# Row order of the left tokens' first-layer values, and the shape of their stores

## The chip, the cores and the metric

The kernel runs on one core of a Trainium2 chip. The core has five engines with instruction queues of their own: PE (TensorE, matrix products), ACT (ScalarE), DVE (VectorE), POOL (GpSimd) and SP (SyncE, which here only issues DMAs), and 16 DMA engines that carry the transfers. Work between the engines is ordered by semaphores. The metric is the device time of one execution, in microseconds.

## The reference

Inputs are q, k and v, each 8 batches x 8 heads x 576 positions x 64 values in float32, and two weight matrices. Attention is computed twice, once over positions averaged in groups of four and once over a band of seven positions, and the two are added. The 4608 tokens of 512 values then go through two layers:

```python
attn_out = out_up + out_local                  # [B, H, S, D]
x = attn_out.transpose(0, 2, 1, 3).reshape(B * S, H * D)   # 4608 x 512
h = x @ w_in                                   # 512 -> 2048
g = h - np.tanh(h)
out = (g @ w_out).astype(np.float32)           # 2048 -> 512, 4608 rows of 2 KB
```

## The kernel before

The attention works on pairs of heads, four pairs to a batch, and leaves its result transposed in `xT` (128 channels by tokens) with the 576 tokens of a batch ordered by (c, g), where token = 4 g + c, c from 0 to 3 and g from 0 to 143. The two layers work on blocks, one block to a batch. A block takes the first 128 values of g, that is 512 tokens. The other 16 values of g, 64 tokens to a batch (`LEFT`), are the *left tokens*: rows 512 to 575 of the batch. Those of two batches are put together into 128 tokens, and handled once for each pair m of batches, four times in all.

First layer of the left tokens (`left1`, e = 0 to 3): L809 makes 16 matmuls into one PSUM bank, four groups of 128 channels by 128 tokens; ACT takes the tanh (L820) into `u`, and DVE subtracts (L822) into `gL`, 128 channels by 16 groups by 128 tokens, in bf16. Those 128 tokens stand in the order (b, c, g): batch, c, g, as they come out of the bank.

Second layer of the left tokens (`left2`): L835 uses each group of `gL` as weights, 128 tokens by 128 channels, against `w_out`; so the order of the tokens in `gL` is the order of the partitions of the result. L846 copies that result, 128 partitions by 512 values, into the tile `keep0`. Then SP issues two stores (L851), one for each batch of the pair, of 64 partitions of `keep0`.

`keep0` is also the place where the second layer of the large blocks keeps a partial result. From the second block on that layer is done as seven products (`product`, L1003) of half the size with sums of blocks ahead of and behind them. The product n = 1 is copied from PSUM to `keep0` (`copy` at L1024, on ACT); the product n = 2 adds onto the same PSUM bank and so comes after that copy. Results of later products are added to `keep0` by POOL (L1074) and DVE (L1027). The copy at L1024 may write `keep0` only when the two stores at L851 have read it.

All operations are put into a list (`op`) with what they read and write; the order in which each engine gets them is a fixed list of turns (`TURNS`), written out in the kernel, and so are the choice of engine and the bank. Each engine works through its queue in order. SP's queue holds the loads of q, k and v (L326, L338, L350, L358, L365), the transposing DMAs (L529, L535, L760), the stores of y (L893) and those of `keep0` (L851). Buffers of loads come free when a cast or a sum on another engine has read them.

Of the kernel before, what the change touches and what calls it, by code (L numbers as in the profile page):

```python
# [10 lines left out]
ALU = mybir.AluOpType  # L11
# [3 lines left out]
class Plan:  # L15
# [13 lines left out]
    def op(self, eng, ns, fn, reads=(), writes=(), port=False, opens=None, uses=(),  # L29
           choice=None, rows=128, share=0.4):  # L30
        i = len(self.ops)
        deps = set()
        for key in reads:
            if key in self.last_write:
                deps.add(self.last_write[key])
        for key in writes:
            if key in self.last_write:
                deps.add(self.last_write[key])
            deps.update(self.readers.get(key, ()))
        for key in reads:  # L40
            self.readers.setdefault(key, set()).add(i)
        for key in writes:
            self.last_write[key] = i
            self.readers[key] = set()
        deps.discard(i)
        if opens and not isinstance(opens, list):
            opens = [opens]
        names = set(uses) | {o[0] for o in opens or ()}
        if choice:
            letter = self.engines[self.choices]  # L50
            self.choices += 1
            eng, ns, fn, port = next(a[:4] for a in choice if a[0][0] == letter)
        self.ops.append((fn, deps, opens or (), names))
        return i
# [34 lines left out]
def kernel(  # L89
# [11 lines left out]
    Dm, Dff = moe_w_in.shape  # L101
# [8 lines left out]
    NBLK, NR, LEFT = B, 3, S - 512  # L110
# [104 lines left out]
    def fixed(name, shape, dt, n=None, pool=const):  # L215
        if n is None:
            return pool.tile(shape, dt, name=name, tag=name)
        return [pool.tile(shape, dt, name=f"{name}{i}", tag=f"{name}{i}")
                for i in range(n)]
# [39 lines left out]
    u = fixed("u", [128, 512], FP32, 3)  # L259
# [7 lines left out]
    gL = fixed("gL", [128, N_FF, 2 * LEFT], BF16)  # L267
# [4 lines left out]
    op = P.op  # L272
    V, A, T, GP = nc.vector, nc.scalar, nc.tensor, nc.gpsimd

    def at(name):
        c = P.place[name]
        return bank[:, c[0]:c[-1] + 1, :]
# [523 lines left out]
    def left1(m, e):  # L801

        name, us = ("hl", m, e), (2 * m * (N_FF + 2) + 2 * N_FF + e) % 3
        s0, f0 = m % 2, 4 * e

        def mm(fs):
            for f in fs:
                for dc in range(N_DC):
                    T.matmul(at(name)[:, 0, 128 * f:128 * f + 128],  # L809
                             w_in_sb[:, dc, (f0 + f) * 128:(f0 + f) * 128 + 128],  # L810
                             xT[dc].rearrange("p (b c g) -> p b c g", b=NR, c=4)[:, s0:s0 + 2, :, 128:G],
                             start=(f == 0 and dc == 0), stop=(dc == N_DC - 1),
                             skip_group_check=True)
        for n in range(2):
            op("PE", 432, lambda n=n: mm(range(2 * n, 2 * n + 2)),
               reads=[("w_in", e)] + [("xs", s0 + i, j) for i in range(2) for j in range(N_DC)],
               writes=[("hld", m, e)] + (["turn1"] if n == 0 else []),
               opens=(name, TAIL if m == NBLK // 2 - 1 else DENSE) if n == 0 else None,
               uses=[name])
        op("ACT", 600, lambda: A.activation(out=u[us], in_=at(name)[:, 0, :], func=AF.Tanh),  # L820
           reads=[("hld", m, e)], writes=[("u", us)], uses=[name])
        op("DVE", 690, lambda: V.tensor_tensor(  # L822
            out=gL[:, f0:f0 + 4, :],
            in0=at(name)[:, 0, :].rearrange("p (f c) -> p f c", c=128),
            in1=u[us].rearrange("p (f c) -> p f c", c=128), op=ALU.subtract),
           reads=[("hld", m, e), ("u", us)], writes=[("gL", e)],
           uses=[name])

    def left2(m):

        name = ("yl", m)

        def mm(e):
            for fc in range(2 * e, 2 * e + 2):
                T.matmul(at(name)[:, 0, :], gL[:, fc, :], w_out_sb[:, fc, :],  # L835
                         start=(fc == 0), stop=(fc == N_FF - 1))
        for e in range(8):
            op("PE", 432, lambda e=e: mm(e),
               reads=[("w_out", e // 2), ("gL", e // 2)],
               writes=[("yld", m)] + (["turn2"] if e == 0 else []),  # L840
               opens=(name, TAIL if m == NBLK // 2 - 1 else DENSE) if e == 0 else None,
               uses=[name])
            if e % 2:
                yield
        op(None, 0, None, choice=[
            ("ACT", 590, lambda: A.copy(out=keep0, in_=at(name)[:, 0, :]), False),  # L846
            ("DVE", 680, lambda: V.tensor_copy(out=keep0, in_=at(name)[:, 0, :]), False, 0)],
           reads=[("yld", m)], writes=[("keep", 0)], uses=[name])
        for n in range(2):
            row = out[(2 * m + (n + m) % 2) * S + 512]  # L850
            op("SP", 450, lambda n=n, row=row: nc.sync.dma_start(  # L851
                out=bass.AP(tensor=row.tensor, offset=row.offset, ap=[[Dm, 4], [4 * Dm, LEFT // 4], [1, Dm]]),
                in_=keep0[LEFT * n:LEFT * n + LEFT, :]),
               reads=[("keep", 0)], writes=[("ylq", n)])
            op("DMA", 6.2 * LEFT, None, reads=[("keep", 0), ("ylq", n)])
# [231 lines left out]
    def second(kb):  # L1087
        if kb % 2:
            yield from left2(kb // 2)
        if not SEVEN[kb]:  # L1090
            for i in range(16):
                mm2(kb, i)
                yield
            return
        if kb == SEVEN.index(True):
            weight_sums()
        token_sums(kb, (0, 2))
        for n in ORDER7[kb == NBLK - 1]:
            yield from product(kb, n)
            if n < 3:  # L1100
                token_sums(kb, (2 * n - 1,))

    def dense(kb):
        steps = iter(()) if kb == 0 else second(kb - 1)
        count = 0 if kb == 0 else 16 + 12 * SEVEN[kb - 1] + 4 * (kb % 2 == 0)
        done, most = 0, 16 + 4 * (kb % 2)
        for i in range(most):
            if kb < NBLK:
                if i < 16:
                    mm1(kb, i)  # L1110
                else:
                    left1(kb // 2, i - 16)
            while done < (i + 1) * count // most:
                next(steps, None)
                done += 1
        for _ in steps:
            pass
# [66 lines left out]
    for p in range(NPAIR):  # L1184
# [16 lines left out]
        if p % NP == NP - 1:  # L1201
            b = p // NP
# [41 lines left out]
```

## Time and profile before

| | us |
|---|---|
| median of 3 runs | 329.01 |
| range of the runs | 328.72 to 329.73 |
| the profiled execution | 328.62 |
| its span, first to last instruction | 326.9 |
| PE busy | 304.2 (93%) |
| DVE busy | 263.4 (81%) |
| ACT busy | 210.5 (64%) |
| POOL busy | 177.7 (54%) |
| 8 stores at L851, issue on SP, each | 0.54 to 0.65 |
| 16 subtractions at L822, all | 10.7 |

The profile is of one execution. Its busy times come from the records of the instructions; a busy PE is not PE at its peak. A row of a group reads: line, engine, operation, what it writes and reads with shapes, count; then busy time in all and the mean in ns of one; then the engine's idle time before these instructions, and what ended it. A row of the chain reads: start, duration, what. "Landing" is the time from the issue of a DMA to the last arrival at its semaphore. PE's granted clock was 0.993 of full speed over the span.

### The profile page before, as it was taken

How to read it: one execution, taken by the hardware profiler on the slowest of the kernel's cores; microseconds unless marked ns; L12 is line 12 of the kernel's file. 1: busy time of each engine (PE TensorE's matmuls, PEld its weight loads, DVE VectorE, ACT ScalarE, POOL GpSimd, SP SyncE). 2: the span in 40 equal slices, each digit the busy share in tenths (PEclk: the TensorE clock that was granted, in tenths of full speed). 3: DMA queues.
4: the chain of work that ended last, by engine and by line, in shares of the span. 5: the costliest groups of instructions: out<-in, count | busy, mean ns of one | idle time of the engine just before them, and what ended most of it. 6: DMA issues, size and time to landing. Idle time of an engine off the chain costs nothing.

```text
span 326.9 us, 7852 instructions
## 1 busy us (share of the span) xinstructions
PE 304.2 (93%) x3001; PEld 201.6 (62%) x3014; DVE 263.4 (81%) x463; ACT 210.5 (64%) x380; POOL 177.7 (54%) x221
## 2 busy tenths in 40 slices
PE   7878999999998999899997999899997998999984
PEld 3675555555766665577676656755766457855773
DVE  3877886898899888999896689998995689746943
ACT  3877876578785797875754788478845774336400
POOL 6167873077684676838752969363931996410000
PEclk9989999999999999999999999999999999999999
DMA  7999999999995899997998796498948320540114
GB/s 222 266 268 230 231 214 166 266 233 209 251 267 145 167 259 257 287 204 187 218 256 167 173 238 190 126 247 136 334 126 137 68 54 39 80 150 0 66 32 128
DMA packets 114852, 59.62 MB, mean 182 GB/s; under 512 B 83968, under 2 KB 112128, under 8 KB 114816
## 3 DMA queue, kind: packets, MB, share of 16 engines
q1 hardware_dynamic: 109472, 52.77, 68.4%
q0 software_dynamic: 4704, 5.77, 9.9%
q10 hardware_dynamic: 640, 0.59, 0.6%
q8 instruction: 23, 0.38, 0.5%
q14 instruction: 13, 0.11, 0.1%
HBM read 44.04 MB, written 9.44 MB: 164 GB/s over the span
## 4 chain that ended last, share of the span: by engine, by line
PE 61%; DMA 19%; DVE 10%; ACT 3%; issue 3%; SPq 2%; POOL 0%; ACTq 0%; DVEq 0%
PE ps L782 28%; PE ps L1003 16%; DMA out_dram<-keep 7%; PE ps L809 4%; PE ps L835 4%; DMA vst<-in_v_dram 4%; PE ps L705 3%; DMA w_in_sb<-in_moe_w_in_dram 3%; DVE gT L797 2%; DVE gT L938 2%; PE ps L635 2%; DMA vr<-in_v_dram 2%; DMA st<-in_q_dram 2%; DMA sr<-in_k_dram 1%; PE ps L863 1%
## 5 line engine op out<-in xcount | busy, mean ns | idle before, releaser
L782 PE MATMUL ps<-xT,w_in_sb 128*128 128x512 bf16 x512 | 122.9, 379 | 1.8 <-DVE gT L797 0.8
L797 DVE TENSOR_TENSOR gT<-ps,u 128x512 bf16<-128x512 f32 x128 | 83.6, 683 | 20.8 <-ACT u L794 19.8
L794 ACT ACTIVATE u<-ps 128x512 f32<-128x512 f32 x128 | 73.5, 598 | 36.3 <-PE ps L782 32.6
L1003 PEld LDWEIGHTS <-gT 128*128 128x128 bf16 x672 | 64.3, 98 | 24.4 <-issue 7.1
L782 PEld LDWEIGHTS <-w_in_sb 128*128 128x128 bf16 x512 | 47.8, 98 | 49.3 <-issue 2.0
L1003 PE MATMUL ps<-w_out_sb,gT 128*128 128x256 bf16 x336 | 43.2, 273 | 5.6 <-ACT keep L1024 5.0
L1003 PE MATMUL ps<-Tw,gT 128*128 128x256 bf16 x336 | 42.1, 273 | 3.5 <-DVE gT L938 2.1
L484 POOL CAST qr<-st 128x512 bf16<-128x512 f32 x40 | 27.8, 703 | 17.5 <-DVE kt L546 4.2
L577 POOL TENSOR_TENSOR qkd<-half 128x288 bf16<-128x288 f32 x25 | 23.5, 941 | 20.4 <-DVE half L572 19.4
L656 ACT ACTIVATE E<-ps 128x912 bf16<-128x912 f32 x32 | 29.9, 935 | 3.5 <-PE ps L635 1.8
L723 DVE TENSOR_TENSOR ln<-ps,r 128x768 bf16<-128x768 f32 x32 | 30.5, 954 | 0.9
L1074 POOL TENSOR_TENSOR y<-y,keep 128x512 f32<-128x512 f32 x12 | 16.9, 1406 | 19.1 <-ACT y L1024 19.1
L691 DVE TENSOR_TENSOR E<-E,mask 128x1152 bf16<-128x1152 bf16 x27 | 24.5, 914 | 2.9 <-ACT E L656 1.6
L705 PEld LDWEIGHTS <-E 128*128 128x128 bf16 x576 | 22.1, 98 | 5.7 <-DVE E L691 1.3
L562 ACT COPY kt<-kq 128x576 bf16<-128x576 bf16 x20 | 23.8, 1189 | 2.0 <-DMA kq<-qr 2.0
L572 POOL TENSOR_TENSOR half<-kq 128x576 f32<-128x576 bf16 x13 | 17.1, 1315 | 14.6 <-ACT kq L557 6.9
L664 ACT ACTIVATE E<-ps 128x576 bf16<-128x576 f32 x32 | 20.9, 653 | 4.7 <-PE ps L651 4.7
L1024 ACT COPY y<-ps 128x512 f32<-128x512 f32 x19 | 11.1, 587 | 19.2 <-PE ps L1003 17.5
L938 DVE TENSOR_TENSOR gT<-gT 128x2048 bf16<-128x2048 bf16 x14 | 19.8, 1415 | 2.9 <-PE ps L1003 2.8
L741 POOL TENSOR_TENSOR xT<-lT 128x336 bf16<-128x336 bf16 (+1 forms) x24 | 17.4, 748 | 5.0 <-DMA lT<-ln 4.9
L705 PE MATMUL ps<-vw,E 128*128 128x65 bf16 x320 | 19.3, 195 | 0.6 <-DVE E L691 0.6
L705 PE MATMUL ps<-vpr,E 128*128 128x65 bf16 x128 | 16.5, 195 | 0.0
(122 smaller groups left out, 489.6 us busy)
## 6 DMA issues: line engine op xcount, KB each, us to landing
vst<-in_v_dram SPq DMA_DIRECT2D x64, 160.0 KB, 4.9
st<-in_k_dram SPq DMA_DIRECT2D x32, 256.0 KB, 3.4
st<-in_q_dram SPq DMA_DIRECT2D x32, 256.0 KB, 6.2
out_dram<-y SPq DMA_DIRECT2D x14, 512.0 KB, 5.0
v<-in_v_dram SPq DMA_DIRECT2D x14, 256.0 KB, 4.6
w_in_sb<-in_moe_w_in_dram POOLq DMA_DIRECT2D x4, 512.0 KB, 9.2
w_out_sb<-in_moe_w_out_dram POOLq DMA_DIRECT2D x4, 512.0 KB, 10.7
v<-in_v_dram POOLq DMA_DIRECT2D x6, 256.0 KB, 4.4
```

The lines of the kernel that those rows point to most:

```text
L484: (eng, ns, lambda dst=dst, src=src, fn=fn: fn(out=dst, in_=src), port)
L562: ("ACT", 1180, lambda: A.copy(out=ktv, in_=src), False),
L577: eng.tensor_tensor(out=pooled, in0=half[:, 0:288].rearrange("p (n x) -> p n x", n=2), in1=half[:, 288:576].rearrange("p (n x) -> p n x", ...
L656: A.activation(out=E[s][:, :, E0:E0 + 456], in_=at(s1)[:, :, PS0:512], func=AF.Exp, scale=SCALE)
L691: eng.tensor_tensor(out=el, in0=el, in1=mask.unsqueeze(1).to_broadcast([128, 2, S]), op=ALU.mult)
L705: T.matmul(po[:, hh, 65 * n:65 * n + 65], E[s][:, hh, e:e + 128], vv, start=start, stop=stop)
L723: op("DVE", 960, lambda: V.tensor_tensor(out=ln[s].rearrange("p n (h d) -> p h n d", d=D), in0=blocks()[:, :, :, 0:64], in1=r[s].unsqueeze ...
L782: T.matmul(at(name)[:, 0, :], w_in_sb[:, dc, fc * 128:(fc + 1) * 128], xT[dc][:, c0:c0 + S].rearrange("p (c g) -> p c g", c=4)[:, :, 0:128 ...
L794: op("ACT", 600, lambda: A.activation(out=u[us], in_=at(name)[:, 0, :], func=AF.Tanh), reads=[("hd", kb, fc)], writes=[("u", us)], uses=[n ...
L797: op("DVE", 690, lambda: V.tensor_tensor(out=gT[g][:, fc, :], in0=at(name)[:, 0, :], in1=u[us], op=ALU.subtract), reads=[("hd", kb, fc), ( ...
L938: eng.tensor_tensor(out=dst[:, fs], in0=x0[:, fs], in1=x1[:, fs], op=ALU.subtract if sub else ALU.add)
L1003: T.matmul(dst, left[:, f, 128 * j:128 * j + 128], right[:, f, :], start=(first and e == 0 and f == 0 and (j == 0 or apart)), stop=(e == 1 ...
```

## The change

Two places change. In `left1` the subtraction at L822 writes `gL` with the tokens ordered (b, g, c), so that token 4 g + c of a batch stands at place 4 g + c of its 64; the inputs are read in the order in which they stand, and of what is written 16 neighbours in that order lie 4 elements (8 bytes) apart. In `left2` the target of a store becomes 64 rows of 2 KB that follow each other, partition by partition; before it was 4 groups of 16 rows, the groups one row apart and the rows of a group four rows apart. The values that are written to each row of the output are the same. The order of instructions on every engine is the same in both kernels, and so is their number; the forms of 16 instructions on DVE and of 8 on SP differ.

```diff
         op("DVE", 690, lambda: V.tensor_tensor(
-            out=gL[:, f0:f0 + 4, :],
-            in0=at(name)[:, 0, :].rearrange("p (f c) -> p f c", c=128),
-            in1=u[us].rearrange("p (f c) -> p f c", c=128), op=ALU.subtract),
+            out=gL[:, f0:f0 + 4, :].rearrange("p f (b g c) -> p (f b) c g", b=2, c=4),
+            in0=at(name)[:, 0, :].rearrange("p (x c g) -> p x c g", c=4, g=16),
+            in1=u[us].rearrange("p (x c g) -> p x c g", c=4, g=16), op=ALU.subtract),
             reads=[("hld", m, e), ("u", us)], writes=[("gL", e)],
             uses=[name])
...
         for n in range(2):
             row = out[(2 * m + (n + m) % 2) * S + 512]
             op("SP", 450, lambda n=n, row=row: nc.sync.dma_start(
-                out=bass.AP(tensor=row.tensor, offset=row.offset, ap=[[Dm, 4], [4 * Dm, LEFT // 4], [1, Dm]]),
+                out=bass.AP(tensor=row.tensor, offset=row.offset, ap=[[Dm, LEFT], [1, Dm]]),
                 in_=keep0[LEFT * n:LEFT * n + LEFT, :]),
                reads=[("keep", 0)], writes=[("ylq", n)])
```

## The prediction

> **What bounds the kernel now.** The page's first part comes first: PE is busy 93% of the span of 326.9 us, DVE 81%, ACT 64%. So a change is worth what it takes out of PE's idle time, and the chain that ended last tells where other work holds PE up. Its shares by engine and line:
>
> ```profile
> PE 61%; DMA 19%; DVE 10%; ACT 3%; issue 3%; SPq 2%; POOL 0%; ACTq 0%; DVEq 0%
> PE ps L782 28%; PE ps L1003 16%; DMA out_dram<-keep 7%; PE ps L809 4%; PE ps L835 4%; DMA vst<-in_v_dram 4%; PE ps L705 3%; DMA w_in_sb<-in_moe_w_in_dram 3%; DVE gT L797 2%; DVE gT L938 2%; PE ps L635 2%; DMA vr<-in_v_dram 2%; DMA st<-in_q_dram 2%; DMA sr<-in_k_dram 1%; PE ps L863 1%
> ```
>
> The third entry is the store that is changed. In the chain in order of time (start, duration, what) it stands four times, always with the same neighbours; the reader is to see that a 0.59 us copy into keep0 starts the moment the second store has landed:
>
> ```profile
> 98.39 5.89 DMA out_dram<-keep
> 104.38 0.59 ACT keep L1024
> ...
> 172.41 6.24 DMA out_dram<-keep
> 178.75 0.59 ACT keep L1024
> ...
> 243.14 4.93 DMA out_dram<-keep
> 248.14 0.59 ACT keep L1024
> ...
> 310.97 4.47 DMA out_dram<-keep
> 315.60 0.59 ACT keep L1024
> ```
>
> Then who waited for whom, ACT's view first, PE's second (total us, times, longest):
>
> ```profile
> ACT keep L1024 <- DMA out_dram<-keep: 15.0, 4, 5.3
> ```
>
> ```profile
> PE ps L1003 <- ACT keep L1024: 5.0, 4, 2.1
> ```
>
> ACT stands 15.0 us (2.93, 3.28, 3.46, 5.30) because keep0 may not be overwritten while the stores read it; PE stands only 5.0 us of that, since it has other matmuls queued ahead of the product that needs the copy. The timeline of PE gives the four pieces, in brackets:
>
> ```profile
> 105.01 1.03 PE L1003 MATMUL ps<-w_out_sb,gT 128*128 128x256 bf16 x8 [0.35 <-ACT keep L1024]
> ...
> 179.38 1.91 PE L1003 MATMUL ps<-w_out_sb,gT 128*128 128x256 bf16 x16 [2.08 <-ACT keep L1024]
> ...
> 248.77 1.91 PE L1003 MATMUL ps<-w_out_sb,gT 128*128 128x256 bf16 x16 [1.64 <-ACT keep L1024]
> ...
> 316.23 0.60 PE L1003 MATMUL ps<-w_out_sb,gT 128*128 128x256 bf16 x4 [0.94 <-ACT keep L1024]
> ```
>
> **Why the store is slow.** The trace records every arrival at a DMA's semaphore. A load of 128 partitions shows 16 arrivals of data. Each of the eight stores from keep0 shows one at about 1.0 us, when no data has moved, and four more: 4.71, 4.74, 5.63 and 6.24 us after the issue at 172.41. The vr load, whose source pattern begins with 8 heads, shows one early and eight late. So the store, whose target pattern begins with 4, runs on four of the 16 DMA engines. Its 64 packets of 2,048 bytes take 84 ns each, at a spacing of 80 ns; two stores give each of the four engines 32 packets, 2.6 us. What is queued behind suffers too: the vst load issued at 99.00 has twelve arrivals at 2.25 to 3.21 us and four at 5.15 to 5.83.
>
> **The change, part by part.** (1) The store's target becomes 64 rows side by side, pattern 64x512. The trace has a store of 64 rows, the last but one of y at 323.00: 16 arrivals, the last after 2.25 us. I therefore take 16 engines for the new one: 8 packets per engine for the two stores, 24 fewer, 24 x 0.08 = 1.92 us. Taking only these off (a cautious estimate, the rest of the landing unchanged), the second stores land after 3.97, 4.32, 3.01 and 2.55 us instead of 5.89, 6.24, 4.93 and 4.47. With nothing else in flight the floor is near the 1.8 to 2.4 us of the last y stores.
>
> How early is early enough? PE was ready at the start of its wait, and the copy takes 0.59 us before that:
>
> - first place: PE ready 104.66, so the copy must start by 104.07; store in at 102.36, ACT free (its queue's previous operation ends) at 101.45. Margin 1.7 us.
> - second: PE ready 177.30, copy by 176.71; store in at 176.73, ACT free at 175.46. Margin nothing by this estimate.
> - third: PE ready 247.13, copy by 246.54; store in at 246.15, ACT free at 244.68. Margin 0.4 us.
> - fourth: PE ready 315.29, copy by 314.70; store in at 313.52, ACT free at 310.30. Margin 1.2 us.
>
> So all four waits of PE go: 0.35 + 2.08 + 1.64 + 0.94 = 5.0 us. The other bounds: nothing if the landing stays; and, since the chain passes through all four landings, at most 4 x 1.92 = 7.7 us by the cautious estimate. I take 5.0, because the chain can't be cut shorter than PE's own work, which fills the stretches behind.
>
> The Trainium skill speaks against part of this: "SBUF — State Buffer", section "Door 1: The DMA port swizzle", states that partitions 0 to 63 reach only 8 of the 16 SBUF ports, so 64 partitions move no faster than 32. By that rule a store of 64 rows would run at the rate of 8 engines, 64 packets / 8 x 0.08 = 0.64 us instead of 0.32; the second place would lose about 0.3 us of its 2.08, and the sum would be 4.7 instead of 5.0. No row before shows a 64-row store of 2,048-byte packets on 16 engines, so the trace can't decide.
>
> (2) What is late next, where a wait goes. Second place: behind the product PE has 8 + 2 + 4 score matmuls whose kt, kq and qkd were ready at 175.0 and before; DVE idled 2.76 us and POOL 4.89 us there, both released by this very product or by ACT behind the copy, so all move together. Third: the lT transposes issued at 244.12 and 245.94 landed only at 250.2 and 251.0, against 2.7 us for the one at 239.78; they came after the store was in and move earlier with it. Fourth: from 316.23 to the end PE runs without another wait; the one DVE operation that the last product needs (L938 at 319.07) follows the product before it, so the end moves by the full 0.94. First: DVE idled 1.88 us before 107.41 for ACT, and PE then meets DVE at 139.18, where it waits 1.35 us; part of that may go too. I count nothing for it.
>
> (3) The subtraction at L822 writes gL in rows order: its inner 16 elements stand 4 apart (8 bytes). It is 16 instructions:
>
> ```profile
> L822 DVE TENSOR_TENSOR gL<-ps,u 128x512 bf16<-128x512 f32 x16 | 10.7, 683 | 2.0 <-ACT u L820 2.0
> L546 DVE COPY kt<-rT 128x64 bf16<-128x64 bf16 x7 | 1.7, 244 | 0.0
> L551 DVE COPY kq<-rT 128x64 bf16<-128x64 bf16 x5 | 1.2, 246 | 0.0
> ```
>
> L546 and L551 read the same kind of source; L546 writes 16 elements 4 apart, the new pattern, and L551 writes 16 in a row: 244 and 246 ns. So I take nothing. Bounds: below, -5 ns each, as no f32 instruction of 512 elements is under 678 ns; above, the step between DVE's strided and plain 128x512 reads, L496 688 and L501 418 ns, 0.27 us each, 16 x 0.27 = 4.3 us. Their cover, if it is not nothing: DVE's idle time in the four stretches with L822 (86.5 to 96, 160 to 169, 231.5 to 239.5, 300 to 307.5) is 1.03 + 0.77 + 0.32 + 0.54 = 2.7 us.
>
> (4) SP still issues eight stores, 596 ns each in the median; other stores took 0.33, the vr load 0.66 us. So -2.1 to +0.5 us on SP, whose queue waits for other engines far longer; taken as nothing. PE's and ACT's orders are untouched, and the weight loads from gL still read 128 adjacent columns.
>
> Sum: -5.0 us. The profiled execution took 328.62 us (326.9 of span and 1.7 around it); 328.62 - 5.0 = 323.6. The median of the runs, 329.01, lies 0.4 above it: 324.0.
>
> **Rivals.** (a) More goes: the first place, once ACT is 2.93 us earlier there, also clears PE's wait at 139.18, 5.0 + 1.35 = 6.4 us, 322.6. For: SP's queue waits on ACT there. Against: DVE is 99% busy from 128 to 144 with its own work. 15%.
>
> (b) A new wait takes the place. After the second and third place PE next depends on DVE at 205 and 274 (L938, 2.1 us in two waits). If DVE doesn't come earlier there, 2.08 or both 2.08 and 1.64 are given back: 326.1 to 327.7, say 326.9. Against: DVE had 1.55 us idle in 192 to 200 and 2.13 in 256 to 264, behind tanhs that wait for matmuls. 20%.
>
> (c) The store doesn't land earlier, because what takes time is the writing to memory under load and not the four engines: 329.0. Against: the vst load's twelve against four arrivals. 6%. The Trainium skill's "DMA: Bandwidth & Descriptors", section "Why a DMA increments its semaphore by 16 and not by 1", says that the count of engines is the largest number up to 16 that divides the slowest dimension of both patterns: 4 before, 16 after, which agrees with the arrivals here.
>
> (d) Slower: the scattered write costs DVE a second pass over each element. An element costs (954 - 683) / 256 = 1.06 ns by L723 (768 elements, 954 ns) against L822, so a second pass is 0.54 us, 8.7 us over 16; 2.7 are covered, 6.0 are not, against 5.0 won: 330.0. It decides from (5.0 + 2.7) / 16 = 0.48 us each. Against: L546, though 64 elements are few. The Trainium skill's "SBUF — State Buffer" (same section) holds strides up to 8 bf16 elements to be free. 7%.
>
> **Chances.** My forecast has 52%. Faster by over 0.3% (1 us, about what the runs' spread of 1.0 us lets one tell): forecast, (a) and (b), 0.87. Within it: (c), 0.06. Slower: (d), 0.07. The range runs from the 7.7 us bound, 321.3, to inside (b), 327.2.
>
> **What would show it.** Right: 16 arrivals per store, landing after 2.3 to 4.3 us; the line "ACT keep L1024 <- DMA out_dram<-keep" gone or under 3 us; PE's wait for ACT keep gone; L822 at 683 ns; vst behind the store with no four late arrivals. Wrong: L822 above 1 us; still four arrivals; or PE's waits for DVE L938 grown by about 3.7 us.

## The result and the profile after

| | median, us | ratio to before | 95% interval |
|---|---|---|---|
| change | 325.20 | 0.988 | 0.985 to 0.991 |
| change, second measurement | 324.85 | 0.989 | 0.985 to 0.992 |
| change, third | 325.64 | 0.992 | 0.988 to 0.996 |

Medians, ratios and intervals, here and below, are of each kernel's fast runs; a run that took over 1.5% longer than the fastest of its kernel is left out of them.

By the ratios the kernel became 2.6 to 4.0 us faster, 4.0 in the first measurement; 5.0 were forecast. The page after, first part and chain (a chain line gives shares of the span by engine, then by line):

```profile
PE 307.2 (95%) x3014; PEld 200.3 (62%) x3014; DVE 271.2 (84%) x463; ACT 210.7 (65%) x380; POOL 175.2 (54%) x221
...
PE 65%; DVE 15%; DMA 7%; ACT 4%; issue 4%; POOL 3%; SPq 1%; ACTq 0%; POOLq 0%; DVEq 0%
PE ps L782 29%; PE ps L1003 21%; DVE gL L822 5%; PE ps L705 4%; PE ps L863 4%; DMA w_in_sb<-in_moe_w_in_dram 3%; DVE gT L938 3%; PE ps L835 2%; DMA st<-in_q_dram 2%; PE ps L635 2%; DVE gT L797 2%; DMA sr<-in_k_dram 1%; DMA vst<-in_v_dram 1%; PE ps L809 1%; DVE S L938 1%
```

The store from keep0, 7% of the chain before, is no longer among its entries. In its place stands a line that was not there: the subtraction at L822, 5%. DVE works 7.8 us more than before. The instructions that read or write keep show how the stores now land; ACT's waits follow:

```profile
DMA to landing us min/median/max: 2.3/2.3/2.4
```

```profile
ACT keep L1024 <- DMA out_dram<-keep: 3.9, 2, 3.1
```

The first line counts three of the eight stores; by their arrivals all eight landed after 2.3 to 2.5 us. Each store has 16 arrivals of data at its semaphore in place of four, and ACT stands 3.9 us where it stood 15.0. Who holds PE up now (total us, times, longest):

```profile
PE ps L1003 <- DVE gT L938: 3.6, 4, 1.9
...
PE ps L835 <- DVE gL L822: 1.2, 3, 0.5
...
PE ps L1003 <- DVE gL L822: 0.8, 2, 0.5
```

The 5.0 us of waiting for the copy into keep0 are gone, all four pieces; 2.0 us of waiting for L822 are new, with 0.3 more at L809, and the wait for DVE's L938 is 3.6 in place of 2.1. This last does not come back: in the profile of the third measurement it is 2.1 again, while the waits for L822 are there (1.6 us). The group of L822 gives the reason (busy us, mean ns):

```profile
L822 DVE TENSOR_TENSOR gL<-ps,u 128x512 bf16<-128x512 f32 x16 | 20.1, 1310 | 1.2 <-ACT u L820 1.0
```

1,310 ns where it was 683: 16 x 0.627 = 10.0 us more on DVE (9.4 by the busy time, in which neighbours overlap). The second place in the timeline of all engines (start, duration, engine, line; in brackets the idle time before and its cause) shows both effects:

```profile
169.14 1.27 DVE L822 TENSOR_TENSOR gL<-ps,u 128x512 bf16<-128x512 f32 x1
...
170.47 1.90 PE L835 MATMUL ps<-w_out_sb,gL 128*128 128x512 bf16 x8 [0.39 <-DVE gL L822]
...
172.41 0.59 ACT L846 COPY keep<-ps 128x512 f32<-128x512 f32 x1 [4.83 <-PE ps L835]
173.02 1.17 SPq L851 DMA_DIRECT2D out_dram<-keep  x2
...
176.65 0.58 ACT L1024 COPY keep<-ps 128x512 f32<-128x512 f32 x1
...
178.42 1.91 PE L1003 MATMUL ps<-w_out_sb,gT 128*128 128x256 bf16 x16
```

PE waits 0.39 us for L822 ahead of the store. The store is issued 1.3 us later than before (173.02 against 171.73), but most of that isn't L822's: in this execution PE was granted only 0.82 of its clock from 96 to 104 us, and in the profile of the third measurement, with the same wait (0.45 us), the store is issued at 171.80. Behind it the copy comes before PE asks for it, and the product starts 5.4 us after the store's issue in place of 7.7.

### The profile page after: what moved, and what is told of

It is laid out like the page before. It is cut to its first block, busy times and chain, and to the rows that moved or that the text cites. A ratio compares the mean times of both kernels' runs of the same rounds, so it can differ in the third digit from the quotient of the medians.

```text
span 324.5 us, 7865 instructions
## 1 busy us (share of the span) xinstructions
PE 307.2 (95%) x3014; PEld 200.3 (62%) x3014; DVE 271.2 (84%) x463; ACT 210.7 (65%) x380; POOL 175.2 (54%) x221
## 4 chain that ended last, share of the span: by engine, by line
PE 65%; DVE 15%; DMA 7%; ACT 4%; issue 4%; POOL 3%; SPq 1%; ACTq 0%; POOLq 0%; DVEq 0%
PE ps L782 29%; PE ps L1003 21%; DVE gL L822 5%; PE ps L705 4%; PE ps L863 4%; DMA w_in_sb<-in_moe_w_in_dram 3%; DVE gT L938 3%; PE ps L835 2%; DMA st<-in_q_dram 2%; PE ps L635 2%; DVE gT L797 2%; DMA sr<-in_k_dram 1%; DMA vst<-in_v_dram 1%; PE ps L809 1%; DVE S L938 1%
## 5 line engine op out<-in xcount | busy, mean ns | idle before, releaser
L797 DVE TENSOR_TENSOR gT<-ps,u 128x512 bf16<-128x512 f32 x128 | 83.8, 684 | 18.8 <-ACT u L794 17.8
L1003 PEld LDWEIGHTS <-gT 128*128 128x128 bf16 x672 | 64.3, 98 | 21.3 <-DVE gT L938 5.1
L1003 PE MATMUL ps<-Tw,gT 128*128 128x256 bf16 x336 | 43.5, 276 | 3.9 <-DVE gT L938 3.6
L1003 PE MATMUL ps<-w_out_sb,gT 128*128 128x256 bf16 x336 | 43.3, 273 | 1.2 <-DVE gL L822 0.8
L577 POOL TENSOR_TENSOR qkd<-half 128x288 bf16<-128x288 f32 x25 | 24.3, 972 | 27.4 <-DVE half L572 21.3
L484 POOL CAST qr<-st 128x512 bf16<-128x512 f32 x40 | 28.7, 724 | 15.3 <-DMA st<-in_k_dram 4.7
L723 DVE TENSOR_TENSOR ln<-ps,r 128x768 bf16<-128x768 f32 x32 | 30.6, 955 | 0.9
L822 DVE TENSOR_TENSOR gL<-ps,u 128x512 bf16<-128x512 f32 x16 | 20.1, 1310 | 1.2 <-ACT u L820 1.0
L938 DVE TENSOR_TENSOR gT<-gT 128x2048 bf16<-128x2048 bf16 x14 | 18.5, 1322 | 0.6 <-PE ps L1003 0.5
L741 POOL TENSOR_TENSOR xT<-lT 128x336 bf16<-128x336 bf16 (+1 forms) x24 | 16.6, 713 | 4.1 <-DMA lT<-ln 4.1
```

The source lines that it names most:

```text
L484: (eng, ns, lambda dst=dst, src=src, fn=fn: fn(out=dst, in_=src), port)
L577: eng.tensor_tensor(out=pooled, in0=half[:, 0:288].rearrange("p (n x) -> p n x", n=2), in1=half[:, 288:576].rearrange("p (n x) -> p n x", ...
L723: op("DVE", 960, lambda: V.tensor_tensor(out=ln[s].rearrange("p n (h d) -> p h n d", d=D), in0=blocks()[:, :, :, 0:64], in1=r[s].unsqueeze ...
L797: op("DVE", 690, lambda: V.tensor_tensor(out=gT[g][:, fc, :], in0=at(name)[:, 0, :], in1=u[us], op=ALU.subtract), reads=[("hd", kb, fc), ( ...
L822: op("DVE", 690, lambda: V.tensor_tensor(out=gL[:, f0:f0 + 4, :].rearrange("p f (b g c) -> p (f b) c g", b=2, c=4), in0=at(name)[:, 0, :]. ...
L938: eng.tensor_tensor(out=dst[:, fs], in0=x0[:, fs], in1=x1[:, fs], op=ALU.subtract if sub else ALU.add)
```

## The experiments

In what follows, theory A is that the store on 16 engines wins PE's waits, and that the scattered writes of L822 give part of it back.

**The store's new target alone.** `left2` as changed, `left1` as before.

```diff
-                out=bass.AP(tensor=row.tensor, offset=row.offset, ap=[[Dm, 4], [4 * Dm, LEFT // 4], [1, Dm]]),
+                out=bass.AP(tensor=row.tensor, offset=row.offset, ap=[[Dm, LEFT], [1, Dm]]),
```

> The store's new target alone; gL keeps its old order, so the rows of the left tokens come out permuted within each batch. Theory A (the store on 16 engines wins PE's four waits; DVE's scattered writes, 1.31 us instead of 0.68, give part of it back): L822 at 0.68 us, landing near 2.3 us, no wait of PE for the copy into keep0 nor for gL, 322 to 324 us, clearly under the changed kernel's 325.2. Rival B (the longer subtraction is hidden): 325.2, as the changed kernel. Rival C (much more is won by earlier loads behind the store): under 321.

Ratio 0.977 (0.972 to 0.983), median 319.9 us: about 7.4 us won by the ratio. The output has the rows of the left tokens in another order, as in the next two kernels. L822 was back at 683 ns, the landing 2.4 us in the median (3.7 at most), and this is what is left of PE's waits for other engines at L1003:

```profile
PE ps L1003 <- DVE gT L938: 1.5, 2, 0.8
```

So the longer subtraction is not hidden (rival B falls), and the store is worth more than the 5.0 us of PE's waits. The median lies below the 322 to 324 us of theory A, in the range of rival C. Two of PE's waits of before lie in the stage after the first place and are missing here: 1.35 us for DVE's L797 at 139.18, and 1.3 us for DVE's ln (L723) at 101.6. That earlier loads behind the store are what clears them, as rival C has it, is not shown.

**The new order of gL alone.** The opposite: `left1` as changed, `left2` as before.

> The new order of gL alone; the store keeps its old target pattern of 4 x 16 rows, so the rows come out permuted within each batch. Theory A: four late arrivals per store, second stores landing after 4.5 to 6.2 us, L822 at 1.31 us, PE waits for keep0 and for gL: 1 to 4 us slower than before, 330.3 to 333.3. Rival B (the longer subtraction is hidden): 329.3, as before.

Ratio 1.014 (1.009 to 1.019), median 332.7: slower, by 4.7 us by the ratio. L822 took 1,310 ns, the second stores landed after 4.4 to 6.2 us with four late arrivals, and PE waited for both:

```profile
PE ps L1003 <- ACT keep L1024: 4.2, 3, 2.1
...
PE ps L1003 <- DVE gL L822: 1.2, 2, 0.8
```

The halves add up: 0.977 x 1.014 = 0.991, which lies in the intervals of the second and third measurement of the change and at the edge of the first's.

**Sixteen groups of rows that lie apart.** Is it the count of engines, or that the rows are side by side in memory?

```diff
-                out=bass.AP(tensor=row.tensor, offset=row.offset, ap=[[Dm, 4], [4 * Dm, LEFT // 4], [1, Dm]]),
+                out=bass.AP(tensor=row.tensor, offset=row.offset, ap=[[Dm, 16], [16 * Dm, LEFT // 16], [1, Dm]]),
```

> gL in its old order, and the store's target as 16 groups of 4 rows that lie 16 rows apart: first dimension 16, but no two rows of a group side by side (rows permuted within each batch). Theory A (the count of engines decides): 16 arrivals of data, landing 2.2 to 2.7 us, time within 0.5 us of the store alone. Rival D (rows side by side in memory are what makes it land early): landing over 4 us, time near 329.

Ratio 0.979 (0.974 to 0.984), 16 arrivals, landing 2.3 us in the median (3.1 at most). With rows 16 apart it lands as early as with rows side by side: the first dimension of 16 is what counts, and rival D falls. This is as the Trainium skill has it ("DMA: Bandwidth & Descriptors", "Why a DMA increments its semaphore by 16 and not by 1": the count follows from the slowest dimension).

**The reordering on PE.** Here xT is read in row order as the moving operand.

```diff
-                         xT[dc].rearrange("p (b c g) -> p b c g", b=NR, c=4)[:, s0:s0 + 2, :, 128:G],
+                         xT[dc].rearrange("p (b c g) -> p b g c", b=NR, c=4)[:, s0:s0 + 2, 128:G, :],
```

> The reordering moved to PE: the 256 matmuls of L809 read xT with the 4 values of c innermost (576 bytes... 288 bytes apart) and their bank comes out in row order; DVE writes gL in a row, store as in the change; the output is the reference's. If PE reads scattered columns at its usual rate (L809 56 ns per matmul in sequence): L822 at 0.68 us, time as the store alone, 322 to 324. If it doesn't: at two passes per column 256 x 0.056 = 14 us more on PE, 336 to 338.

Ratio 1.129 (1.123 to 1.134), 370.0 us. PE's group at L809, in this kernel and in that with the store alone:

```profile
L809 PE MATMUL ps<-xT,w_in_sb 128*128 128x128 bf16 x256 | 58.3, 400 | 0.0
```

```profile
L809 PE MATMUL ps<-xT,w_in_sb 128*128 128x128 bf16 x256 | 15.4, 219 | 0.0
```

58.3 / 256 = 228 ns of PE for a matmul in place of 60: nearly four times, where the dearer expectation had twice. The matmuls of a group follow each other by 222 to 224 ns, in stretches in which PE was granted its full clock as well as where it was granted half; with the store alone by 56. L809 takes 42.9 us more. Against the store alone, whose store this kernel has too, the ratios differ by 0.151, some 50 us: all 43 stand on the path, and more. The rest was not measured apart; PE's granted clock was 0.929 over the span here and 0.997 with the store alone.

**The reordering where DVE reads.** Bank and u are read in row order, gL is written in a row.

```diff
-            out=gL[:, f0:f0 + 4, :],
-            in0=at(name)[:, 0, :].rearrange("p (f c) -> p f c", c=128),
-            in1=u[us].rearrange("p (f c) -> p f c", c=128), op=ALU.subtract),
+            out=gL[:, f0:f0 + 4, :].rearrange("p f (b g c) -> p (f b) g c", b=2, c=4),
+            in0=at(name)[:, 0, :].rearrange("p (x c g) -> p x g c", c=4, g=16),
+            in1=u[us].rearrange("p (x c g) -> p x g c", c=4, g=16), op=ALU.subtract),
```

> Store as in the change; the subtraction reads both inputs in row order (bank and u, 4 values 64 bytes apart) and writes gL in a row; the output is the reference's. If it is only scattered writing of bf16 that costs DVE: L822 at 0.68 us, time as the store alone, ratio to before 0.975 to 0.98. If scattered access of any kind costs a second pass: L822 1.2 us or more, ratio as the change's, 0.985 to 0.99, or above.

Ratio 0.984 (0.980 to 0.988); the duration lies between the two that were expected:

```profile
L822 DVE TENSOR_TENSOR gL<-ps,u 128x512 bf16<-128x512 f32 x16 | 15.9, 1014 | 1.4 <-ACT u L820 1.3
```

**ACT orders u.** As the one before, but ACT writes u in row order, and DVE reads only the bank in that order.

```diff
-        op("ACT", 600, lambda: A.activation(out=u[us], in_=at(name)[:, 0, :], func=AF.Tanh),
+        op("ACT", 600, lambda: A.activation(out=u[us].rearrange("p (x g c) -> p x c g", c=4, g=16),
+                                            in_=at(name)[:, 0, :].rearrange("p (x c g) -> p x c g", c=4, g=16), func=AF.Tanh),
```

> Store as in the change; ACT writes the tanh (float32) into u in row order, and DVE reads only the bank in that order; the output is the reference's. If float32 written 16 bytes apart costs ACT nothing (L820 stays at 0.60 us) and DVE's strided read of the bank costs nothing: ratio 0.975 to 0.98. If DVE's read of the bank costs: L822 over 1.0 us and ratio 0.985 or above. If ACT's write costs: L820 over 0.9 us, 16 x 0.3 = 5 us on ACT, which has 36% idle: ratio 0.975 to 0.985.

Ratio 0.984 (0.982 to 0.987). The groups of ACT and of DVE (here the subtraction is on line 823):

```profile
L820 ACT ACTIVATE u<-ps 128x512 f32<-128x512 f32 x16 | 16.8, 1126 | 2.9 <-PE ps L809 2.2 <-DVE gT L797 0.5
```

```profile
L823 DVE TENSOR_TENSOR gL<-ps,u 128x512 bf16<-128x512 f32 x16 | 11.0, 689 | 5.1 <-ACT u L820 4.9
```

So DVE's read of the bank in row order costs next to nothing (689 ns against 683); the read of u in SBUF cost it 1,014 - 689 = 325 ns, and ACT's scattered write of u costs ACT 1,126 - 600 = 526 ns.

**A tile of its own.** The left tokens' result goes to a tile `rows0`, so the wait on keep0 can't arise; the store stays on four engines. Room for the tile is made as the expectation says, with four small copies less at the start.

```diff
+    rows0 = fixed("rows0", [128, 512], FP32)
...
-            ("ACT", 590, lambda: A.copy(out=keep0, in_=at(name)[:, 0, :]), False),
+            ("ACT", 590, lambda: A.copy(out=rows0, in_=at(name)[:, 0, :]), False),
...
-                in_=keep0[LEFT * n:LEFT * n + LEFT, :]),
-               reads=[("keep", 0)], writes=[("ylq", n)])
+                in_=rows0[LEFT * n:LEFT * n + LEFT, :]),
+               reads=[("rows", 0)], writes=[("ylq", n)])
```

> gL and the store's target as before; the left tokens' result is copied to a tile of its own, so that the copy into keep0 never waits for the stores (room made by storing the five selection matrices as windows of one strip of 240 columns, four small copies less at the start); the output is the reference's. Theory A1 (all that the store cost was the wait on keep0): no wait for keep0, landing still 4 to 6 us on four engines, ratio as the store alone, 0.975 to 0.98. Theory A2 (the loads and transposes behind the four busy engines cost too): PE's 5.0 us are won, the rest isn't, ratio 0.983 to 0.987.

Ratio 0.990 (0.987 to 0.992), 3.4 us won: without the wait, but with the slow store (landing after 3.8 to 6.2 us), less than half of the store's gain is had. That is less than theory A2's 0.983 to 0.987 too, so not even the 5.0 us of PE's waits were won. The timeline shows one place where the slow store holds up what comes behind. At the third place, with the stores issued from 239.60 on, the transposes into lT came late, DVE's join waited for them, and PE for the join:

```profile
241.31 3.63 SPq L759 DMA_TRANSPOSE lT<-ln  x2
...
248.75 0.53 DVE L740 TENSOR_TENSOR xT<-lT 128x336 bf16<-128x336 bf16 x2 [2.99 <-DMA lT<-ln]
249.33 0.38 PE L781 MATMUL ps<-xT,w_in_sb 128*128 128x512 bf16 x1 [0.98 <-DVE xT L740]
249.55 0.53 DVE L740 TENSOR_TENSOR xT<-lT 128x336 bf16<-128x336 bf16 x2 [0.28 <-DMA lT<-ln]
250.13 2.10 PE L781 MATMUL ps<-xT,w_in_sb 128*128 128x512 bf16 x9 [0.43 <-DVE xT L740]
```

With the store alone on 16 engines the transposes were issued at 238.27, and the join followed after 4.6 us instead of 7.4 (the two transposes landed after 4.5 and 3.3 us, with the own tile after 7.4 and 6.2):

```profile
242.84 1.12 DVE L741 TENSOR_TENSOR xT<-lT 128x336 bf16<-128x336 bf16 x4 [0.31 <-DMA lT<-ln]
```

**Own tile, stores of 16 rows.** As before it, each store split by c into four.

```diff
-                out=bass.AP(tensor=row.tensor, offset=row.offset, ap=[[Dm, 4], [4 * Dm, LEFT // 4], [1, Dm]]),
+                out=bass.AP(tensor=row.tensor, offset=row.offset + c * Dm, ap=[[4 * Dm, 16], [1, Dm]]),
```

> As the own tile, but each store is issued as four of 16 rows (4 rows apart), each on 16 engines, so no four engines are crowded; SP issues six more DMAs at each place, 6 x 0.55 = 3.3 us. Theory A2: the best correct kernel, ratio 0.972 to 0.98, unless SP's time delays the loads; then 0.98 to 0.987. Theory A1: the same as the own tile.

Ratio 0.987 (0.983 to 0.991). Each store lands 1.7 us after its issue in the median, but SP needs 3.6 us for the eight in place of 1.3. The interval overlaps that of the own tile, so this measurement doesn't tell the two theories apart. The timeline of the own tile speaks for A2, at one place.

**Both engines read the bank.** Reading float32 from PSUM in row order was next to free for DVE; ACT's plain copies from a bank in stride (L496, 590 ns) and in a row (L501, 588 ns) had suggested the same for ACT. (DVE's copies on the same two lines took 688 and 418 ns: of a bank of bf16 DVE did pay for the stride.)

```diff
-        op("ACT", 600, lambda: A.activation(out=u[us], in_=at(name)[:, 0, :], func=AF.Tanh),
+        op("ACT", 600, lambda: A.activation(out=u[us].rearrange("p (x g c) -> p x g c", c=4, g=16),
+                                            in_=at(name)[:, 0, :].rearrange("p (x c g) -> p x g c", c=4, g=16), func=AF.Tanh),
...
-            out=gL[:, f0:f0 + 4, :],
-            in0=at(name)[:, 0, :].rearrange("p (f c) -> p f c", c=128),
-            in1=u[us].rearrange("p (f c) -> p f c", c=128), op=ALU.subtract),
+            out=gL[:, f0:f0 + 4, :].rearrange("p f (b g c) -> p (f b) g c", b=2, c=4),
+            in0=at(name)[:, 0, :].rearrange("p (x c g) -> p x g c", c=4, g=16),
+            in1=u[us].rearrange("p (x g c) -> p x g c", c=4, g=16), op=ALU.subtract),
```

> Store as in the change; ACT's tanh and DVE's subtraction both read the bank in row order (4 values 64 bytes apart) and both write in a row, so nothing in SBUF is scattered; the output is the reference's. If reading a bank in that order is free on both (DVE's was 0.69 us in the kernel where ACT ordered u): L820 at 0.60 us, L822 at 0.69 us, ratio to before 0.972 to 0.98, as the store alone: the full gain with the right rows. If ACT's read costs: L820 over 0.9 us, ratio 0.98 to 0.987.

> The changed kernel once more, on the same chip as the kernel that reads the bank in row order. Theory A: ratio 0.983 to 0.991, 2 to 4 us slower than that kernel. Rival B: no difference between the two.

Ratio 0.984 (0.979 to 0.989) against 0.989 (0.985 to 0.992) for the change: medians 321.9 and 324.9 us, but intervals that overlap, and a ratio above the 0.972 to 0.98 that were expected. Neither engine pays, as their groups show:

```profile
L820 ACT ACTIVATE u<-ps 128x512 f32<-128x512 f32 x16 | 9.3, 600 | 4.2 <-PE ps L809 3.6 <-DVE gT L797 0.4
```

```profile
L823 DVE TENSOR_TENSOR gL<-ps,u 128x512 bf16<-128x512 f32 x16 | 10.7, 684 | 2.0 <-ACT u L820 2.0
```

As written, the patterns of this subtraction have as many dimensions as those of the change; so it is the scattered write, not the form of the patterns, that took 1,310 ns there. Both kernels were measured once more.

> The kernel that reads the bank in row order, once more, since its interval and that of the change overlapped. Theory A: ratio to before 0.975 to 0.985, below the change's on the same chip by 0.005 or more, the two intervals apart or nearly so.

> The changed kernel beside it, on the same chip. Theory A: ratio 0.985 to 0.991. Rival B: the same as the kernel that reads the bank in row order.

Ratio 0.977 (0.972 to 0.982), 320.6 us, against 0.992 (0.988 to 0.996), 325.6 us: apart. This version writes every row where it belongs and, by this second measurement, has the gain of the store alone. It beats both kernels. The change itself came out just above the 0.985 to 0.991 that were expected.

## Why the prediction was right or wrong

The stages between the copies at L846 (the fourth place to the end is the last) leave out the start, whose length differs by a microsecond or two between profiles: the first copy comes at 96.79 us in the first profile of the change and at 98.01 in the third. The first four of the 16 subtractions at L822 lie in it. In us, from the profiled executions; of the change the third measurement is taken, for the clock's sake (1.0 over these stages):

| | 1 to 2 | 2 to 3 | 3 to 4 | 4 to end | sum |
|---|---|---|---|---|---|
| before | 74.04 | 70.73 | 67.86 | 17.20 | 229.83 |
| change (third) | 73.18 | 69.42 | 67.37 | 16.03 | 226.00 |
| store alone | 71.73 | 68.20 | 65.70 | 16.03 | 221.66 |
| order alone | 74.82 | 71.91 | 68.01 | 17.13 | 231.87 |
| own tile | 72.74 | 68.27 | 68.43 | 16.13 | 225.57 |
| bank reads (first) | 71.40 | 68.56 | 66.30 | 16.04 | 222.30 |

Each row is one profile; the first stage of the bank reads was 71.40 us in one profile and 72.48 in the other, so single stages are good to about 1 us. For the order alone the table has 2.0 us more than before, less than the 4.7 of the runs' ratio; its profile is of the fastest of its runs.

The store's mechanism was right: 16 engines, landing 2.3 to 2.5 us (2.3 to 4.3 were allowed), all four of PE's waits gone. The cautious estimate, which took off only the packets' time, was far too cautious under load: at the second place 4.32 us were expected and 2.4 came, presumably because the other traffic no longer queued on those four engines either. The margins were therefore all wide, and the 0.3 us that the prediction set against the second place by the Trainium skill's rule of the 8 ports ("SBUF — State Buffer", "Door 1: The DMA port swizzle") can't be seen. By their records in the traces the packets took 155 ns in the median with the rows side by side, nearly the doubling of the 84 ns that this rule gives, but 85 ns with the rows 16 apart, out of the same 64 partitions; so the partitions that are read are not the reason, and the landing was 2.3 us in both.

The gain from the store was mis-sized. By the table's stages the store alone won 2.31, 2.53, 2.16 and 1.17 us, 8.2 in all, where PE's waits said 0.35, 2.08, 1.64 and 0.94, 5.0 in all; the ratio of the runs says 7.4. The failing step is "I count nothing for it": rival (a), the first place also clearing the wait at 139.18, is what the store alone showed there, with the wait for ln besides. The bound from the chain, 7.7, was nearer than the value taken. And the own tile shows, at the third place, that a store on four engines costs through the transposes behind it too, which the prediction named only as moving along. How the 8.2 divide between these was not measured further.

The step that failed is (3), "So I take nothing": L822 rose by 627 ns, over the upper bound of 270 ns and over the second pass of 540 ns in rival (d). The two means on which it rests, 244 and 246 ns, agree by chance: each is of a few instructions, and one of L551's five took twice as long as the rest. The same lines before the change, with shortest, median and longest duration:

```profile
L546 DVE COPY kt<-rT x7: 225/234/300, 8.0 to 71.9; 128x64 bf16<-128x64 bf16 x7
L546 ACT COPY kt<-rT x5: 326/343/370, 17.1 to 77.2; 128x64 bf16<-128x64 bf16 x5
L551 ACT COPY kq<-rT x7: 298/307/317, 11.2 to 79.6; 128x64 bf16<-128x64 bf16 x7
L551 DVE COPY kq<-rT x5: 203/208/405, 8.5 to 68.8; 128x64 bf16<-128x64 bf16 x5
```

So in the medians L546, which writes 4 apart, took 26 ns longer on DVE and 36 on ACT, and the price was there to be seen. Scaled from 64 to 512 elements DVE's 26 ns would be 0.21 us, a third of what L822 paid. Why it is not more is open. Both lines read SBUF in stride, at 234 / 64 = 3.7 ns an element against 683 / 512 = 1.3 in L822 of before, and part of a slow write may be hidden by a slow read; this was not tested. The rule of the Trainium skill cited there ("SBUF — State Buffer", "Door 1: The DMA port swizzle": strides up to 8 bf16 elements free) does not hold for this instruction: with 4 elements apart it took 1,310 ns in place of 683. The lower bound misread a row too, though nothing hangs on it: DVE's cast at L484 reads 512 float32 elements and takes 498 ns.

Rival (d) had the place and, within 0.09 us, the price of the scattered write (that it is a second pass over each element is not shown), yet its time of 330.0 didn't come. Its point of decision, 0.48 us, was passed and the kernel still became faster, since more was won by the store, and since the path took 4.7 us of the 10.0 (the order alone), not 10.0 less the 2.7 of idle time in the same stretches. How the other half is caught up was not looked into.

So 5.0 forecast and 2.6 to 4.0 measured are near each other by luck, through two errors of opposite sign: 7.4 won where 5.0 were put down, and 3 to 5 given back where nothing was.

Rival (c) fell with the arrivals. Of rival (b), the sign that was named, a wait for L938 grown by 3.7 us, did not come: it was 3.6 us in one profile of the change and 2.1, as before, in another; with the store alone it is 1.5.

## What to carry to other kernels

Look at how many arrivals a DMA has at its semaphore: here a target pattern whose first dimension was 4 used four engines, and delayed not only itself but loads and transposes queued behind it. A reordering has a price that depends on where it is done; here reads of float32 from PSUM took it for nothing, and a scattered write to SBUF nearly doubled the instruction. Before a row is taken as the price of an access pattern, look at the shortest, the median and the longest of its instructions, and at what else in it is slow: a mean of five can hide the price.

## What the runs showed of the hardware

The same order of 128 tokens, done in six places (512 elements per partition unless noted):

| where | plain, ns | in row order, ns |
|---|---|---|
| DVE writes bf16 to SBUF, 8 bytes apart | 683 | 1,310 |
| DVE reads float32 from SBUF, 64 bytes apart (bank also in row order) | 689 | 1,014 |
| ACT writes float32 to SBUF, 16 bytes apart | 600 | 1,126 |
| DVE reads float32 from PSUM, 64 bytes apart | 683 | 684 to 689 |
| ACT reads float32 from PSUM, 64 bytes apart | 600 | 600 |
| PE reads a moving operand of 128 bf16 columns, 288 bytes apart, busy time per matmul | 60 | 228 |

For bf16 in a bank, DVE's copies of 512 elements took 418 ns in a row (L501) and 688 ns with elements 256 bytes apart (L496); ACT's took 588 and 590.

A store of 64 rows of 2 KB landed after 2.3 us in the median on 16 engines whether its rows lay side by side or 16 apart (3.7 at most), and after 3.8 to 6.2 on four. A store of 16 rows of 2 KB on 16 engines landed after 1.7 us in the median.
